# A fused spectral filter and MLP on one core: MLP steps taken two at a time

## The chip, the cores and the metric

The kernel runs on one core of a Trainium2 chip. The core has a matrix engine (TensorE, called PE in the profile, with its weight loads listed apart as PEld), a vector engine (VectorE, DVE), a scalar engine (ScalarE, ACT), GpSimd (POOL) and a queue engine that issues most of the transfers (SyncE, SP). Each engine works through its own list of instructions in order. The matrix engine writes its results into PSUM, of which this kernel uses eight banks of 512 float32 a partition; the other engines read them from there into SBUF.

The metric is the time of one execution on the device in microseconds. The output must agree with the reference in float32 accuracy: large products are made of three matmuls with operands split in a high and a low part.

## The reference

```
X  = rfft(x, axis=1)                       # x: 8 sequences of 3008 tokens, 256 wide
Yr = Xr @ w_r - Xi @ w_i + b_r
Yi = Xr @ w_i + Xi @ w_r + b_i
Y  = soft threshold of Yr and Yi by 0.01
y  = irfft(Y, n=3008, axis=1)
h  = y.reshape(24064, 256) @ w_in          # w_in: 256 x 2048
g  = maximum(0.01 * h, h)
out = g @ w_out                            # w_out: 2048 x 256
```

## The kernel before

The tokens of all sequences are handled in 47 chunks of 512. A sequence first goes through the transform stages: a forward transform in two parts (`fwd`, and `stage_b` in `mid`), the projection by w_r and w_i with bias and threshold (`proj`), and the inverse transform in two parts (`stage_g` in `mid`, and `inverse`), with trips through DRAM between them. `forms` then writes seven combinations of the four quarters of a chunk (two halves of the width by two halves of the tokens), each as a high and a low part (`yh`, `yl`).

The MLP takes a chunk in 8 steps, each for 256 of the 2048 hidden columns; there are 376 steps in all, counted by `i`, and (ci, q) is chunk and step in it. A step has three parts:

- `moe_a`: four of the seven products of a Strassen-like scheme, each three matmuls of 256 columns (L99, 12 matmuls), into two banks b1 and b2 of the PSUM tag `psh`, which has four banks. Then p1 is copied out of b1 (ACT, L614), u2 is summed (DVE, L615), and the first quarter of the activation's input is read out of b2 (DVE, L617 and L618).
- `moe_b`: the other three products (L99, 9 matmuls), into the same two banks. Then the DVE reads b2 for two more quarters (L630), ACT reads b1 through the activation (L632), applies it to the rest in SBUF (L633), and `halves` splits the result in `gh` (ACT, L597) and `gl` (DVE, L599). After L630 and L632 the two banks are free for another step.
- `moe_o`: the second product, for one half `eh` of the output columns, 6 matmuls of 512 columns (L646) from `gh` and `gl` into a bank of the tag `pso`, where all 8 steps of a chunk add up. After the last step of a chunk ACT copies the bank out (L651) and SP issues its transfer to DRAM (L652).

For the first chunk (`DIRECT = 1`) `moe_a` makes the plain products (12 matmuls of 512 columns) and `moe_b` does nothing.

The order in which each engine gets its instructions is set when the program is built, by a planner that goes through a simulated time: an engine takes the instruction that stands first in the traced program among those whose inputs and buffers are ready. Two things bind it. `in_order` queues every matmul of a part behind the matmul that was traced last in the part before, so the parts of the MLP follow each other in the order of the calls; within that bound single products may be put off. And the transform's TensorE work in the stage functions is queued behind the last MLP matmul traced at that point (`issue_after(mlp[0].ins)`).

`moe` is a generator. At each `yield` it gives its place in chunks, and the loop at the end of the kernel (L794 to L810) traces as much of the transforms of the next sequences as is due by that place. `tokens` traces the loads, the inverse transforms and `forms` of the next chunk in portions, one at each `next(nxt, None)`. Step i traces: moe_a of step i, moe_b of step i-1, a stop for the transforms, the second half of moe_o of step i-3, the first half of moe_o of step i-2, another stop. In the order of TensorE this is a, b, o, o for each step.

Buffers that bear on it: `psh` four banks, `pso` two and `psf` two (transforms); `gf`, `gh` and `gl` two buffers each; `u2` two, `p1` one.

Of the kernel before, what the change touches and what calls it, by code (L numbers as in the profile page):

```python
# [31 lines left out]
def spectral_mlp_kernel(  # L32
# [23 lines left out]
    NH = D // P  # L56
    NPAIR = NK1 // 2
    NQ = NF // 2
    NT, HT = 512, 256
    NV = 2 * NG * N1  # L60
    CS = 512
    LAG = 2
    PAUSE = 10 * CS
    DIRECT = 1
    SHARE = 1.7
# [25 lines left out]
    def in_order(part, *args):  # L91

        with tc.issue_after(mlp[0].ins) if mlp else nullcontext():
            part(*args)
# [559 lines left out]
    steps = [(ci, q) for ci in range(nch) for q in range(NQ)]  # L654
# [8 lines left out]
    def tokens(ci):  # L663

        yield
        for p in due[ci]:
            v_load(p)
        for _ in range(3):
            yield
        for eh in range(NH):  # L670
            for p in due[ci]:
                with tc.issue_after(mlp[0].ins):
                    inverse(p, eh)
                yield
        yield from forms(ci)

    def moe():

        for i, (ci, q) in enumerate(steps):
            if q == 0:  # L680
                nxt = tokens(ci + 1) if ci + 1 < nch else iter(())
            in_order(moe_a, ci, q)
            if i >= 1:
                in_order(moe_b, *steps[i - 1])
            next(nxt, None)
            yield ci + (q + 0.5) / NQ
            if i >= LAG + 1:
                in_order(moe_o, *steps[i - LAG - 1], 1)
            if i >= LAG:
                in_order(moe_o, *steps[i - LAG], 0)  # L690
            next(nxt, None)
            if q == NQ - 1:
                for _ in nxt:
                    pass
            yield ci + (q + 1) / NQ
        in_order(moe_o, *steps[-LAG - 1], 1)
        in_order(moe_b, *steps[-1])
        for s in steps[-LAG:]:
            for eh in range(NH):
                in_order(moe_o, *s, eh)  # L700

    class Stream:
        def __init__(self, gen, total):
# [90 lines left out]
    for i, pos in enumerate(moe()):  # L794
        if i % 2 == 0 and len(converted) < NQ:
            with tc.issue_after(made[0].ins), tc.issue_after(made[1].ins):
                next(wout, None)
        while cur + 1 < NB - 1 and pos >= (read[cur + 1] if cur >= 0 else 0):
            for s in streams:
                s.finish()  # L800
            cur += 1
            streams = ([Stream(fwd(cur + 1), (FWD + 4 * CS) * SHARE)] if cur else []) + [mids[cur]]
        frac = (pos - read[cur]) / (read[cur + 1] - read[cur]) if cur + 1 < NB else 1
        if cur == 0:
            frac = max(0, frac - 0.2) * 1.25
        work = frac / 0.95 * sum(s.total for s in streams)
        with tc.issue_after(converted[-1].ins) if cur == 0 else nullcontext():
            for s in streams:
                s.to(work / s.total)
                work = max(0, work - s.total)  # L810
# [106 lines left out]
```

## Time and profile before

| | us |
|---|---|
| median of three runs | 2535.69 |
| lowest and highest | 2535.54, 2536.94 |
| the profiled execution | 2536.52 |
| its span, first to last instruction | 2534.7 |
| PE busy | 2495.6 |
| DVE busy | 1872.9 |
| ACT busy | 1663.1 |

Busy times are unions of an engine's instructions. A matmul's duration in the profile is longer than the distance to the next one, since they overlap; distances are read from the starts. In the groups of a page the columns are busy time, mean duration in ns, and the idle time of the engine just before such instructions with what ended it.

### The profile page before, as it was taken

To read this page: it belongs to the slowest core of one execution; us is meant where nothing else is said; L and a number is where in the kernel's file an instruction comes from. 1 tells how busy PE (TensorE), PEld (TensorE's weight loads), DVE (VectorE), ACT (ScalarE), POOL (GpSimd) and SP (SyncE) were. 2 spreads that over 40 slices of the span, in tenths; PEclk is the share of its full clock that TensorE was granted. 3 is DMA by queue.
4 is the path that set the end of the run, shared out by engine and by line. 5 is a ranking of instruction groups with operands and counts; after the bars stand their busy time and mean duration, and the time that the engine had idled before them with its cause. 6 is when DMAs were issued, how large, how long until landed. Compare 5 with 4: busy or idle time off the path is not lost.

```text
span 2534.7 us, 42316 instructions
## 1 busy us (share of the span) xinstructions
PE 2495.6 (98%) x16180; PEld 2246.0 (89%) x16180; DVE 1872.9 (74%) x3460; ACT 1663.1 (66%) x3152; POOL 122.2 (5%) x96
## 2 busy tenths in 40 slices
PE   6999999999999999999999999999999999999999
PEld 4588888999899998999989999899998999999998
DVE  7886777777877778777777777877778777667665
ACT  4876765667666765667656676666765677656564
POOL 0000000000000000000000000000000010000000
PEclk8999999999999999999999999999999999999999
DMA  8621132111321113221132111321114211100000
GB/s 268 196 82 47 46 96 77 46 51 45 96 73 51 54 38 91 69 58 50 42 95 69 51 50 42 103 69 53 44 38 113 64 54 42 41 21 29 21 14 17
DMA packets 117803, 165.05 MB, mean 65 GB/s; under 512 B 13513, under 2 KB 69345, under 8 KB 117601
## 3 DMA queue, kind: packets, MB, share of 16 engines
q1 hardware_dynamic: 76228, 112.34, 14.6%
q10 hardware_dynamic: 41373, 50.01, 7.7%
q8 instruction: 127, 2.08, 0.3%
q14 instruction: 75, 0.61, 0.1%
HBM read 86.59 MB, written 75.71 MB: 64 GB/s over the span
## 4 chain that ended last, share of the span: by engine, by line
PE 93%; DMA 3%; ACT 2%; DVE 1%; issue 1%; SPq 0%; ACTq 0%; DVEq 0%
PE pso L646 40%; PE psh L99 35%; PE psf L85 11%; PE psf L518 3%; PE psf L373 3%; DMA xin<-x_dram 1%; DMA u_dram<-xin 1%; PE psh L85 0%; DMA u<-u_dram 0%; DVE gl L599 0%; DMA raw<-w_out_dram 0%; DMA bias<-b_i_dram 0%; ACT zf L429 0%; PE psh L373 0%; DMA win_raw<-w_in_dram 0%
## 5 line engine op out<-in xcount | busy, mean ns | idle before, releaser
L99 PE MATMUL psh<-yh,win_hi 128*128 128x256 f32 (+1 forms) x2608 | 728.7, 281 | 1.1 <-DVE gf L630 0.5
L99 PE MATMUL psh<-yl,win_hi 128*128 128x256 f32 (+1 forms) x2608 | 728.5, 280 | 0.0
L99 PE MATMUL psh<-yh,win_lo 128*128 128x256 f32 (+1 forms) x2608 | 723.5, 279 | 0.0
L599 DVE TENSOR_TENSOR gl<-gf,gh 128x1024 fp32r<-128x1024 f32 x376 | 461.3, 1227 | 299.8 <-ACT gh L597 289.6
L646 PE MATMUL pso<-gh,wout_hi 128*128 128x512 f32 x1504 | 592.9, 394 | 0.5 <-ACT ob L651 0.5
L646 PE MATMUL pso<-gl,wout_hi 128*128 128x512 f32 x1504 | 590.2, 392 | 1.3 <-DVE gl L599 1.3
L646 PE MATMUL pso<-gh,wout_lo 128*128 128x512 f32 x1504 | 589.3, 392 | 0.0
L99 PEld LDWEIGHTS psh<-yh,win_hi 128*128 128x128 f32 x2608 | 488.5, 188 | 19.6 <-DVE gf L630 2.2
L99 PEld LDWEIGHTS psh<-yl,win_hi 128*128 128x128 f32 x2608 | 490.2, 188 | 16.8 <-DVE yl L545 0.3
L99 PEld LDWEIGHTS psh<-yh,win_lo 128*128 128x128 f32 x2608 | 488.9, 188 | 1.9
L633 ACT ACTIVATE gf<-gf 128x768 f32<-128x768 f32 x368 | 311.8, 847 | 216.6 <-DVE gf L630 205.6
L597 ACT CAST gh<-gf 128x1024 fp32r<-128x1024 f32 x376 | 395.0, 1051 | 35.2 <-PE pso L646 25.9
L646 PEld LDWEIGHTS pso<-gl,wout_hi 128*128 128x128 f32 x1504 | 282.7, 188 | 63.0 <-DVE gl L599 4.0
L646 PEld LDWEIGHTS pso<-gh,wout_hi 128*128 128x128 f32 x1504 | 283.1, 188 | 47.0 <-ACT ob L651 0.9
L646 PEld LDWEIGHTS pso<-gh,wout_lo 128*128 128x128 f32 x1504 | 283.0, 188 | 46.5
L632 ACT ACTIVATE gf<-psh 128x256 f32<-128x256 f32 x368 | 142.2, 386 | 233.1 <-PE psh L99 225.3
L630 DVE TENSOR_TENSOR gf<-psh,u 128x512 f32<-128x512 f32 x368 | 252.4, 686 | 47.8 <-PE psh L99 46.3
L614 ACT COPY p<-psh 128x256 f32<-128x256 f32 x368 | 137.5, 374 | 143.9 <-PE psh L99 131.8
L411 POOL TENSOR_TENSOR kb<-bias,kc 128x512 f32<-128x512 f32 x84 | 119.5, 1423 | 2046.8 <-ACT kc L409 1800.4
L615 DVE TENSOR_TENSOR u<-psh,p 128x256 f32<-128x256 f32 x368 | 154.6, 420 | 32.9 <-ACT p L614 31.0
L617 DVE TENSOR_TENSOR gf<-psh,u 128x256 f32<-128x256 f32 x368 | 154.8, 421 | 21.1 <-PE psh L99 7.2
L618 DVE TENSOR_TENSOR gf<-psh,gf 128x256 f32<-128x256 f32 x368 | 154.5, 420 | 4.9
(124 smaller groups left out, 3124.5 us busy)
## 6 DMA issues: line engine op xcount, KB each, us to landing
u<-u_dram SPq DMA_DIRECT2D x192, 128.0 KB, 2.7
v_dram<-v ACTq DMA_DIRECT2D x192, 128.0 KB, 2.4
out_dram<-ob SPq DMA_DIRECT2D x94, 256.0 KB, 2.0
vin<-v_dram SPq DMA_DIRECT2D x96, 240.0 KB, 3.5
xin<-x_dram SPq DMA_DIRECT2D x78, 240.0 KB, 2.9
u_dram<-xin ACTq DMA_DIRECT2D x72, 240.0 KB, 2.4
raw<-w_out_dram SPq DMA_DIRECT2D x8, 512.0 KB, 4.7
win_raw<-w_in_dram SPq DMA_DIRECT2D x7, 512.0 KB, 6.8
```

Of the source, the lines that this page charges most:

```text
L85: last = nc.tensor.matmul(dst, a, b, start=(i == 0), stop=(i == len(terms) - 1))
L99: mlp[:] = [nc.tensor.matmul(dst, a, b, start=start and i == 0, stop=i == 2, skip_group_check=True)]
L597: cp = act.copy(gh, g)
L599: parted[:] = [cp, dve.tensor_sub(gl, g, gh.bitcast(F32))]
L614: act.copy(p1, b1[:, lo])
L615: dve.tensor_add(u2, b1[:, hi], p1)
L617: dve.tensor_add(g[:, 3], b2[:, hi], u2)
L618: dve.tensor_add(g[:, 3], b2[:, lo], g[:, 3])
L630: dve.tensor_add(g[:, 1:3], b2.rearrange("p (k n) -> p k n", k=2), u2.unsqueeze(1).broadcast_to([P, 2, HT]))
L632: act.activation(g[:, 0], b1[:, lo], AF.Prelu, alpha=SLOPE)
L633: act.activation(g[:, 1:4], g[:, 1:4], AF.Prelu, alpha=SLOPE)
L646: mlp[:] = [nc.tensor.matmul(po, a[:, f, s], r[:, i], start=(f == 0 and j == 0), stop=(f == NF - 1 and j == 2),)]
```

## The change

The steps are traced in pairs. For a pair i, i+1 the order of the calls becomes: moe_a of step i, moe_b of step i-1, a stop for the transforms, moe_a of step i+1, moe_b of step i, a stop, then both halves of moe_o of step i-2, a stop, both halves of moe_o of step i-1, a stop. In the order of TensorE this is a, b, a, b, o, o, o, o for two steps. The number of stops and the places that they give are the same, in the same sequence. The end of the generator follows suit: moe_b of the last step, then moe_o of the last two. The constant `LAG` is gone.

```diff
-        for i, (ci, q) in enumerate(steps):
+        def seconds(i):
+
+            for eh in range(NH):
+                in_order(moe_o, *steps[i], eh)
+
+        for i in range(0, len(steps), 2):
+            ci, q = steps[i]
             if q == 0:
                 nxt = tokens(ci + 1) if ci + 1 < nch else iter(())
-            in_order(moe_a, ci, q)
-            if i >= 1:
-                in_order(moe_b, *steps[i - 1])
-            next(nxt, None)
-            yield ci + (q + 0.5) / NQ
-            if i >= LAG + 1:
-                in_order(moe_o, *steps[i - LAG - 1], 1)
-            if i >= LAG:
-                in_order(moe_o, *steps[i - LAG], 0)
-            next(nxt, None)
-            if q == NQ - 1:
-                for _ in nxt:
-                    pass
-            yield ci + (q + 1) / NQ
-        in_order(moe_o, *steps[-LAG - 1], 1)
+            for k in range(2):
+                in_order(moe_a, *steps[i + k])
+                if i + k:
+                    in_order(moe_b, *steps[i + k - 1])
+                next(nxt, None)
+                yield ci + (q + (k + 1) / 2) / NQ
+            for k in range(2):
+                if i:
+                    seconds(i + k - 2)
+                next(nxt, None)
+                if k and q == NQ - 2:
+                    for _ in nxt:
+                        pass
+                yield ci + (q + (k + 3) / 2) / NQ
         in_order(moe_b, *steps[-1])
-        for s in steps[-LAG:]:
-            for eh in range(NH):
-                in_order(moe_o, *s, eh)
+        seconds(-2)
+        seconds(-1)
```

More of the change, by code (lines that the diff above doesn't have):

```diff
@@ L61, in spectral_mlp_kernel @@
     CS = 512
-    LAG = 2
     PAUSE = 10 * CS
```

## The prediction

> **What bounds the kernel now.** I read the page first, then the slices of 100 us, then the chain of waits, then the timeline around the change.
>
> ```profile
> span 2534.7 us, 42316 instructions
> PE 2495.6 (98%) x16180; PEld 2246.0 (89%) x16180; DVE 1872.9 (74%) x3460; ACT 1663.1 (66%) x3152; POOL 122.2 (5%) x96
> PEclk8999999999999999999999999999999999999999
> ```
>
> ```profile
> 0.00:100.00 100.00, 74.11 (x301) 51.68 (x302) 76.02 (x128) 59.37 (x110) 0.77 (x6) 0.93 0.79 230
> 200.00:300.00 100.00, 98.92 (x666) 90.43 (x665) 68.77 (x129) 67.09 (x134) 10.24 (x7) 0.98 0.17 48
> 1000.00:1100.00 100.00, 100.00 (x660) 90.86 (x659) 74.34 (x145) 63.58 (x122) 2.82 (x2) 1.00 0.26 77
> 2300.00:2400.00 100.00, 100.00 (x649) 90.78 (x648) 66.72 (x118) 59.46 (x99) 0.00 (x0) 1.00 0.07 21
> ```
>
> In the second fence the columns are the stretch, then the busy time of PE, PEld, DVE, ACT and POOL, the granted clock, the DMA share and GB/s. TensorE is idle for 39 us of 2534.7, and 26 of these lie in the first 100 us, ahead of most of the MLP. From then on it is full. So the change can gain next to nothing by closing gaps; it can only open some, or make the matmuls themselves follow each other faster.
>
> How fast they follow is read best where the transforms are over, in the chain of waits near 2303 us, one row for the first products and one for the second:
>
> ```profile
> 2303.24 2.41 PE psh L99 x21
> 2305.65 2.73 PE pso L646 x12
> ```
>
> One step costs 2.41 + 2.73 = 5.14 us of TensorE: 12 matmuls of moe_a, 9 of moe_b, 12 of moe_o. How many steps each stage holds follows from the second-product matmuls, 12 a step (first row); the second row is all of TensorE's work in the same stretch, the third the end stage:
>
> ```profile
> 311.50:2176.00 1864.50, 851.80 (x3398) 613.41 (x3399) 1.00 0.22 62
> 311.50:2176.00 1864.50, 1862.62 (x12358) 1697.70 (x12358) 1402.32 (x2630) 1242.67 (x2396) 107.27 (x80) 1.00 0.22 62
> 2176.00:2530.00 354.00, 196.15 (x808) 146.29 (x808) 1.00 0.07 23
> ```
>
> 3398 / 12 = 283 steps in the transform stage, each 1864.5 / 283 = 6.59 us, so 1.45 us a step is transform work; 808 / 12 = 67 steps in the end stage; 376 - 283 - 67 = 26 before, of which 8 are the direct ones without moe_b.
>
> **What the change moves.** It adds and removes no instruction. Per pair the queue goes from a, b, o, o, a, b, o, o to a, b, a, b, o, o, o, o. What counts is what each matmul run must wait for, and how much MLP work lies in front of it.
>
> *The banks of psh.* A step takes two of the four, from its moe_a until L630 (DVE, reads b2) and L632 (ACT, reads b1) of its moe_b are done. When a(i+1) starts, step i holds two, and step i-1 held the others: a(i+1) waits for L630 and L632 of b(i-1). Before, twelve second products stood between b(i-1) and a(i+1). After, nothing of the MLP does in the second step of each pair. The end stage shows the price, for the step whose nine b matmuls end at 2305.37:
>
> ```profile
> 2303.07 0.28 PE L99 MATMUL psh<-yh,win_hi 128*128 128x256 f32 x1
> 2303.67 0.28 PE L99 MATMUL psh<-yh,win_lo 128*128 128x256 f32 x1
> 2303.98 0.37 ACT L614 COPY p<-psh 128x256 f32<-128x256 f32 x1 [1.13 <-PE psh L99]
> 2304.80 0.28 PE L99 MATMUL psh<-yh,win_hi 128*128 128x256 f32 x1
> 2305.34 0.69 DVE L630 TENSOR_TENSOR gf<-psh,u 128x512 f32<-128x512 f32 x1
> 2305.37 0.28 PE L99 MATMUL psh<-yh,win_lo 128*128 128x256 f32 x1
> 2305.49 0.39 PE L646 MATMUL pso<-gh,wout_hi 128*128 128x512 f32 x1
> 2305.68 0.39 ACT L632 ACTIVATE gf<-psh 128x256 f32<-128x256 f32 x1 [1.33 <-PE psh L99]
> 2305.95 0.42 DVE L618 TENSOR_TENSOR gf<-psh,gf 128x256 f32<-128x256 f32 x1
> 2308.22 0.28 PE L99 MATMUL psh<-yh,win_hi 128*128 128x256 f32 x1
> ```
>
> TensorE could issue its next matmul at 2305.49. L632 ends at 2306.07 and L630 at 2306.03. What lies between such an end and the matmul that waited for it is seen here:
>
> ```profile
> 1005.45 1.22 DVE L599 TENSOR_TENSOR gl<-gf,gh 128x1024 fp32r<-128x1024 f32 x1
> 1006.80 0.41 PE L646 MATMUL pso<-gl,wout_hi 128*128 128x512 f32 x1
> ```
>
> ```profile
> PEld pso L646 <- DVE gl L599: 4.0, 8, 1.0
> ```
>
> In the timeline the weight load before that second row is marked as released by L599, whose end is 1006.67, so 0.13 us. In the new order a(i+1) would start at 2306.07 + 0.13 = 2306.20 instead of 2305.49: a gap of **0.71 us a pair** where nothing else is there to be issued. Today the next a comes only at 2308.22, 2.15 us after L632; that is the cover the change takes away. In the end stage the only other TensorE work are the inverse transforms of L518, four groups of eight in 100 us against ten pairs; I count no cover there (columns as above, L518 alone):
>
> ```profile
> 2300.00:2400.00 100.00, 4.22 (x32) 4.05 (x32) 1.00 0.07 21
> ```
>
> That makes 67 / 2 = 33 pairs x 0.71 = **23 us**.
>
> *The same in the transform stage.* Here the DVE also carries transforms, and L630 queues behind them. First and last step of the stage:
>
> ```profile
> 311.54 0.28 PE L99 MATMUL psh<-yh,win_lo 128*128 128x256 f32 x1
> 311.85 0.39 ACT L632 ACTIVATE gf<-psh 128x256 f32<-128x256 f32 x1 [0.31 <-PE psh L99]
> 313.72 0.68 DVE L630 TENSOR_TENSOR gf<-psh,u 128x512 f32<-128x512 f32 x1
> 2175.49 0.28 PE L99 MATMUL psh<-yh,win_lo 128*128 128x256 f32 x1
> 2175.83 0.68 DVE L630 TENSOR_TENSOR gf<-psh,u 128x512 f32<-128x512 f32 x1
> 2176.01 0.38 ACT L632 ACTIVATE gf<-psh 128x256 f32<-128x256 f32 x1
> ```
>
> From the end of the group's last matmul to the end of L630 it is 2.58 us in the first, 0.74 in the last; over all 284 groups of 21 in this stretch the mean is 1.15 (median 0.89), and for L632 0.29 (median 0.42). The b1 half of a(i+1), six matmuls or 0.70 us, can run once L632 is done and covers part of L630. Taken group by group (the earlier of the two, or the later less 0.70, whichever is more, with 0.075 us for the release and 0.165 because a matmul is issued that much before its predecessor's end), the gap averages 1.04 us. Against this stands that L630 will queue less: today L599 of the step before, 1227 ns, often stands ahead of it, and after the change that one belongs to the previous pair and ran during four halves of second products. I take 0.85, between the end stage's 0.71 and 1.04.
>
> ```profile
> L599 DVE TENSOR_TENSOR gl<-gf,gh 128x1024 fp32r<-128x1024 f32 x376 | 461.3, 1227 | 299.8 <-ACT gh L597 289.6
> L630 DVE TENSOR_TENSOR gf<-psh,u 128x512 f32<-128x512 f32 x368 | 252.4, 686 | 47.8 <-PE psh L99 46.3
> ```
>
> ```profile
> DVE gf L630 <- PE psh L99: 46.3, 65, 2.1
> PE psh L99 <- DVE gf L630: 0.5, 1, 0.5
> ```
>
> The last fence is from the table of waits (us in total, times, longest): only 65 of the 368 L630 found the DVE idle, and a's matmuls waited for one of them once.
>
> What can fill the gap is transform work: what is traced behind b(i-1) is queued behind its last traced matmul, so it becomes issuable just there. In the present trace a transform matmul stands directly behind 30% of the 284 groups, as after this one:
>
> ```profile
> 1014.51 2.42 PE psh L99 x21
> 1016.93 0.71 PE psf L85 x3
> ```
>
> Laid over the gaps, such matmuls fill 0.29 us of the 1.04 on the mean. So 0.85 - 0.30 = 0.55 us a pair: 283 / 2 = 142 pairs x 0.55 = **78 us**, and (26 - 8) / 2 = 9 earlier pairs, **5 us**. The bounds: all filled, 0 (then 5 us less as well); nothing filled at 1.04, 151 pairs = 157 us. I stay nearer the latter since 70% of groups have no transform matmul behind them and nothing of the MLP may pass: the second products are queued behind b(i), b(i) behind a(i+1).
>
> *The waits that become tighter or looser.* b(i), second of the pair, needs L618(i). In the end stage L618 ends 2306.37 - 2303.07 = 3.30 us after its a starts; b(i) comes 2.41 + 0.71 + 1.38 = 4.5 us after it: covered. If L618 is late, the three products of b1 and the second products pass. o(i-1) needs gl(i-1), from L599; for the first and the last group above that is
>
> ```profile
> 317.53 1.22 DVE L599 TENSOR_TENSOR gl<-gf,gh 128x1024 fp32r<-128x1024 f32 x1
> 2178.51 1.23 DVE L599 TENSOR_TENSOR gl<-gf,gh 128x1024 fp32r<-128x1024 f32 x1 [0.73 <-ACT gh L597]
> ```
>
> It ends 5.4 us after the group's last matmul on the mean of the 284, 7.3 us at the 95th percentile. On TensorE 0.7 of gap, 2.41 x 12 / 21 = 1.38 of a(i+1), 1.03 of b(i), 2.73 of o(i-2) and two matmuls, 0.46, lie between, 6.3 us, or 7.7 with the 1.45 of transforms: I count nothing; without the transforms a tenth of the pairs would lose up to 1 us, 18 us in all, for the upper bound. Buffers of gf, gh and gl (two each) come free later only for the second step, whose next reader is a whole run away. The output copies and their DMA move by half a step at most and the token loads on SP's queue keep their place among the four stops of a pair; nobody on the path waits for them.
>
> *The gain.* After a change from second to first products the first five matmuls come 0.120 us apart (2303.07 to 2303.67), the last five 0.114 (2304.80 to 2305.37): 0.03 us for each change. 180 of 368 changes go: **-6 us**. Beyond that no more than the 39 us of idle time could be gained, and nearly all of it lies in the head, which the change does not touch.
>
> Sum: 23 + 78 + 5 - 6 = 100 us. The profiled execution took 2536.5, its span 2534.7, the median of the runs is 2535.7; 2535.7 + 100 = **2636 us**, 3.9% slower. About 0.2%, 5 us, is what can be told from no change here.
>
> **The rivals.**
> 1. *Transforms fill every gap of their stage.* For it: they are 1.45 us a step, far more than the gap, and the planner takes whatever is ready. Against it: the 30%. Only the end stage pays: 23 - 6 = +17, 2553 us. Chance 0.14.
> 2. *Nothing fills, and gl is late too.* For it: DVE at 74% overall and only 65 of 368 L630 found it idle. 23 + 157 + 18 - 6 = +192, 2728 us. Chance 0.15.
> 3. *Not slower.* L630 and L632 would have to end before a(i+1) is due, or the planner would have to put 0.71 us of other work in front of it also in the end stage; then only the faster succession remains, 2536 - 6 = 2530 us. It decides from a release within 0.12 us of the last matmul on, and no row shows ACT's 0.39 us fitting there. Chance 0.05, with the case that the planner dissolves the pairs and nothing changes, 2536.
> 4. *The clock falls.* The first slice, with TensorE 74% busy, had 0.93 of the clock, the slice from 200 us, 99% busy, 0.98; those read from 300 us on 1.00. Gaps every 11 us at 0.98 over some 2400 us add 49 us to the forecast, 2685; at 0.93, 181 us, 2817. Against it: each gap is under 1 us. Chance 0.04. The Trainium skill, TensorE: Matmul & The Clock Gate, section "A second HAM failure mode: psum-queue depth-cycling", speaks for this one: frequent short idling between groups that cycle through banks made the clock gate swing. No slice of this trace shows it so far.
>
> **How the numbers follow.** The forecast has 0.62, the rivals 0.14, 0.15, 0.05 and 0.04. The range goes from 2552, which takes in most of rival 1, to 2722, the forecast with nothing filled at 1.04 us (2716) and a part of rival 2: 0.60 + 0.11 + 0.08 + 0.02, about 8 in 10. Slower by over 0.2%: 0.93; within 0.2%: 0.04; faster: 0.03.
>
> **What would show it.** In the chain of waits: pieces of 12 + 9 + 12 + 9 first products and 24 second ones in the end stage, with a wait of PE for L632 or L630 after the first 21, about 0.7 us each, 33 times; in the table of waits "PE psh L99 <- ACT gf L632" and "<- DVE gf L630" up from the 0.5 us above to 50 to 150 us. The slices from 2300 us fall from 100 to about 94 busy, those of the transform stage to about 96. If the end stage stays at 100, the bank argument is wrong; if it falls and the transform stage stays at 100, rival 1 holds; a PEclk below 1.00 after 300 us would be rival 4; waits of L646 for L599 of over 20 us, rival 2.

## The result, and the profile after

The changed kernel takes 2628.6 us in the median (four runs, 2624.8 to 2631.8) beside 2535.6 us for the kernel before on the same chip: 1.0367 times as long, 95% interval 1.0354 to 1.0380. The forecast was 2636 us. The profiled execution took 2628.4 us, its span is 2626.0.

The page after, its first lines and the groups that answer to those of before. One line fewer stands ahead of them in the code, so L99 is now L98, and likewise L645 is moe_o, L629 the DVE's reading of b2, L631 ACT's reading of b1, L598 makes gl.

```profile
span 2626.0 us, 42169 instructions
PE 2535.8 (97%) x16180; PEld 2259.3 (86%) x16180; DVE 1866.9 (71%) x3460; ACT 1654.8 (63%) x3152; POOL 117.2 (4%) x96
...
L98 PE MATMUL psh<-yh,win_hi 128*128 128x256 f32 (+1 forms) x2608 | 748.4, 287 | 52.4 <-DVE gf L629 26.2
...
L629 DVE TENSOR_TENSOR gf<-psh,u 128x512 f32<-128x512 f32 x368 | 252.4, 686 | 126.8 <-PE psh L98 124.8
```

TensorE has the same 16180 matmuls. Ahead of the first matmul of a product (the yh, win_hi row) it now stands idle for 52.4 us, where it was 1.1, as the same row of the page before shows:

```profile
L99 PE MATMUL psh<-yh,win_hi 128*128 128x256 f32 (+1 forms) x2608 | 728.7, 281 | 1.1 <-DVE gf L630 0.5
```

The table of waits after names who ended them (us in total, times, longest):

```profile
PE psh L98 <- DVE gf L629: 26.2, 41, 3.2
PE psh L98 <- ACT gf L631: 23.0, 49, 1.0
...
PE pso L645 <- DVE gl L598: 5.3, 13, 2.1
```

These are the two instructions that free a step's banks. One pair of the end stage, in rows picked from the timeline (start, duration, what, idle before and its releaser):

```profile
2380.23 0.69 DVE L629 TENSOR_TENSOR gf<-psh,u 128x512 f32<-128x512 f32 x1
2380.26 0.28 PE L98 MATMUL psh<-yh,win_lo 128*128 128x256 f32 x1
2380.57 0.38 ACT L631 ACTIVATE gf<-psh 128x256 f32<-128x256 f32 x1 [1.33 <-PE psh L98]
2380.98 0.38 PE L98 MATMUL psh<-yh,win_hi 128*128 128x256 f32 x1 [0.44 <-DVE gf L629]
2381.20 0.28 PE L98 MATMUL psh<-yl,win_hi 128*128 128x256 f32 x1
```

The last b matmul starts at 2380.26, the next first product at 2380.98: 0.72 us, of which 0.114 is the ordinary distance. And the chain of waits there, in order of time:

```profile
2380.23 0.70 DVE gf L629
2380.93 0.04 issue
2380.98 1.98 PE psh L98 x15
2382.96 1.38 PE pso L645 x6
2384.33 0.71 PE psh L98 x6
2385.05 4.09 PE pso L645 x18
2389.14 0.73 PE psh L98 x6
```

Behind the gap the planner does not keep the run of first products whole: six matmuls of the pair's second moe_b come only after six second products.

Where the 91 us of span went can be worked out from the starts of all matmuls in the two timelines: what a distance exceeds 114 ns after a matmul of 256 columns, 227 ns after one of 512 and 112 ns after one of 128 or 64 (the medians). Summed by the kind of matmul that came late, in us, with the distances that are less than 0.15 us too long in a column of their own:

| stage | late first products | late second products | late transforms | under 0.15 us each |
|---|---|---|---|---|
| transform stage, before (150 to 2180) | 1.4 | 3.2 | 3.8 | 23.6 |
| transform stage, after (150 to 2254) | 53.4 | 11.4 | 1.1 | 39.7 |
| end stage, before | 0.0 | 0.9 | 0.0 | 2.5 |
| end stage, after | 15.4 | 0.9 | 0.0 | 5.7 |

Together 35 us before and 128 us after; the first 150 us differ by less than 1. Of the 92 us between them 67 lie in first products that came late, 8 in second ones and 19 in the short ones; transforms give 3 back.

Most of the short ones belong to the waits too. In the rows above the matmul behind the one that waited follows it by 0.22 us and not by 0.114, and so it is behind each of the 102 late first products of this trace, by 0.11 us in the median: 11 of the 19 us. A wait costs its gap and 0.11 us more.

### The profile page after: what moved, and what is told of

It is laid out like the page before. It is cut to its first block, busy times and chain, and to the rows that moved or that the text cites. A ratio compares the mean times of both kernels' runs of the same rounds, so it can differ in the third digit from the quotient of the medians.

```text
span 2626.0 us, 42169 instructions
## 1 busy us (share of the span) xinstructions
PE 2535.8 (97%) x16180; PEld 2259.3 (86%) x16180; DVE 1866.9 (71%) x3460; ACT 1654.8 (63%) x3152; POOL 117.2 (4%) x96
## 4 chain that ended last, share of the span: by engine, by line
PE 79%; DVE 9%; ACT 6%; DMA 4%; issue 2%; ACTq 0%; SPq 0%; DVEq 0%
PE pso L645 34%; PE psh L98 28%; PE psf L84 10%; PE psf L517 3%; PE psf L372 2%; DVE gf L629 2%; DMA xin<-x_dram 2%; DVE gl L598 1%; DMA u_dram<-xin 1%; ACT zf L428 1%; DVE u L614 1%; ACT gf L631 1%; ACT zf L424 1%; DVE t L418 1%; ACT gf L632 1%
## 5 line engine op out<-in xcount | busy, mean ns | idle before, releaser
L98 PE MATMUL psh<-yh,win_hi 128*128 128x256 f32 (+1 forms) x2608 | 748.4, 287 | 52.4 <-DVE gf L629 26.2
L98 PE MATMUL psh<-yl,win_hi 128*128 128x256 f32 (+1 forms) x2608 | 730.6, 280 | 0.0
L98 PE MATMUL psh<-yh,win_lo 128*128 128x256 f32 (+1 forms) x2608 | 729.3, 280 | 0.0
L598 DVE TENSOR_TENSOR gl<-gf,gh 128x1024 fp32r<-128x1024 f32 x376 | 460.0, 1223 | 228.1 <-ACT gh L596 227.1
L645 PE MATMUL pso<-gl,wout_hi 128*128 128x512 f32 x1504 | 591.2, 393 | 5.8 <-DVE gl L598 5.3
L645 PE MATMUL pso<-gh,wout_hi 128*128 128x512 f32 x1504 | 592.5, 394 | 0.5 <-ACT gh L596 0.5
L645 PE MATMUL pso<-gh,wout_lo 128*128 128x512 f32 x1504 | 590.3, 392 | 0.0
L98 PEld LDWEIGHTS psh<-yh,win_hi 128*128 128x128 f32 x2608 | 489.5, 188 | 93.4 <-ACT gf L631 37.5
L98 PEld LDWEIGHTS psh<-yl,win_hi 128*128 128x128 f32 x2608 | 490.6, 188 | 14.4 <-DVE yl L544 0.3
L98 PEld LDWEIGHTS psh<-yh,win_lo 128*128 128x128 f32 x2608 | 490.7, 188 | 1.8
L632 ACT ACTIVATE gf<-gf 128x768 f32<-128x768 f32 x368 | 312.2, 848 | 259.4 <-DVE gf L629 239.6
L645 PEld LDWEIGHTS pso<-gl,wout_hi 128*128 128x128 f32 x1504 | 283.1, 188 | 70.5 <-DVE gl L598 13.0
L629 DVE TENSOR_TENSOR gf<-psh,u 128x512 f32<-128x512 f32 x368 | 252.4, 686 | 126.8 <-PE psh L98 124.8
L645 PEld LDWEIGHTS pso<-gh,wout_hi 128*128 128x128 f32 x1504 | 283.5, 188 | 49.8 <-ACT gh L596 1.3
L645 PEld LDWEIGHTS pso<-gh,wout_lo 128*128 128x128 f32 x1504 | 283.3, 188 | 48.7
L631 ACT ACTIVATE gf<-psh 128x256 f32<-128x256 f32 x368 | 142.5, 387 | 152.6 <-PE psh L98 149.6
```

Source lines behind the costliest of these rows:

```text
L98: mlp[:] = [nc.tensor.matmul(dst, a, b, start=start and i == 0, stop=i == 2, skip_group_check=True)]
L598: parted[:] = [cp, dve.tensor_sub(gl, g, gh.bitcast(F32))]
L629: dve.tensor_add(g[:, 1:3], b2.rearrange("p (k n) -> p k n", k=2), u2.unsqueeze(1).broadcast_to([P, 2, HT]))
L631: act.activation(g[:, 0], b1[:, lo], AF.Prelu, alpha=SLOPE)
L632: act.activation(g[:, 1:4], g[:, 1:4], AF.Prelu, alpha=SLOPE)
L645: mlp[:] = [nc.tensor.matmul(po, a[:, f, s], r[:, i], start=(f == 0 and j == 0), stop=(f == NF - 1 and j == 2),)]
```

## The experiments

The theory was that the four banks of psh set the loss: the second step's moe_a directly follows the moe_b whose banks it needs, and the transforms fill part of the gap. The main rival was that the pairing loses by its bursts: four halves of moe_o in a row want gl earlier, and DVE and ACT get their work in lumps. All runs (each interval is the ratio to the kernel before on the same chip):

| run | median us | against before, 95% interval |
|---|---|---|
| changed kernel | 2628.6 | 1.0354 to 1.0380 |
| moe_b's b1 product first, changed kernel | 2623.5 | 1.0330 to 1.0364 |
| the same, kernel before | 2543.5 | 1.0021 to 1.0045 |
| one half of moe_o between | 2562.1 | 1.0094 to 1.0125 |
| fifth bank for psh, one for pso | 2573.1 | 1.0137 to 1.0167 |
| its control, one bank for pso | 2628.6 | 1.0357 to 1.0388 |
| both halves together, not paired | 2556.6 | 1.0068 to 1.0098 |
| transforms traced at the gap alone | 2574.9 | 1.0141 to 1.0172 |
| transforms traced behind the first moe_o alone | 2681.4 | 1.0561 to 1.0597 |
| transforms at one stop a step, kernel before | 2558.3 | 1.0079 to 1.0106 |
| one half between, and transforms at that gap | 2544.8 | 1.0023 to 1.0049 |
| b, b, a, a, o, o, o, o | 2669.8 | 1.0510 to 1.0539 |
| the same, shifted by a step | 2619.8 | 1.0312 to 1.0340 |

**A fifth bank, and its control.** The output banks give one up: both halves of the columns are summed in one, so these two kernels leave the separate halves out. The diff shows the two lines that matter; the other users of the two tags, and the copies of the output, follow suit.

```diff
-            o_t[ci, eh] = bank("pso", 2)
+            o_t[ci, eh] = o_t[ci, 0] if eh else bank("pso", 1)
...
-        b1, b2 = bank("psh", 4), bank("psh", 4)
+        b1, b2 = bank("psh", 5), bank("psh", 5)
```

> The changed kernel with psh at five banks and pso at one: both halves of the output columns are summed in the same bank, so the output holds their sum twice; the copies and transfers of a chunk are all made after its last second product. Bank theory: the second step's a takes the free bank at once and needs one more only 0.70 us later; the gap in the end stage disappears, the waits of L98 for L631 and L629 fall below 10 us, and the time to 2545 to 2565 us (what is left is the wait for gl). Rival (bursts): 2620 to 2635 us, as with the one bank less alone.

> The control for the fifth bank: pso at one bank with the same sum of both halves, psh at four as in the changed kernel. Both theories: as the changed kernel, 2620 to 2640 us, if the single pso bank costs nothing by itself; what it differs from that is the price of the merging, to be taken off the run with five banks.

The control took 2628.6 us, as the changed kernel; with five banks it is 2573.1. So **one more bank takes away 55 us of the 93**. The end stage is full again, which it is not in the control's case (194.11 of 200 us); here the stretch of 2300 to 2500 us in the changed kernel, then with five banks (columns as in the prediction):

```profile
2300.00:2500.00 200.00, 194.15 (x1245) 174.70 (x1245) 129.50 (x234) 112.44 (x199) 0.00 (x0) 1.00 0.07 24
```

```profile
2300.00:2500.00 200.00, 200.00 (x1303) 182.50 (x1303) 136.89 (x245) 114.63 (x206) 0.00 (x0) 1.00 0.07 22
```

Waits of first products for L629 or L631 fall from 49.2 to 1.4 us. It is 8 us above what was expected; another wait grew, that for gl, threefold.

```profile
PE pso L645 <- DVE gl L598: 15.8, 20, 1.0
```

**Cover between the two.** One of the four halves of moe_o goes back between the first step's moe_b and the second step's moe_a.

```diff
                 yield ci + (q + (k + 1) / 2) / NQ
+                if i and k == 0:
+                    in_order(moe_o, *steps[i - 2], 0)
             for k in range(2):
                 if i:
-                    seconds(i + k - 2)
+                    for eh in range(1 - k, NH):
+                        in_order(moe_o, *steps[i + k - 2], eh)
```

> The changed kernel with one of the four halves of moe_o (6 matmuls, 1.38 us) put back between the first step's b and the second step's a: a, b, o, a, b, o, o, o. Bank theory: the banks are released 0.5 us after b in the end stage and 1.3 us on the mean in the transform stage, so the waits of L98 for L631 and L629 (49 us for the matmuls alone) go to under 15 us; gl of the later step is needed as early as before, so some wait of L645 for L598 stays, 5 to 20 us: 2545 to 2565 us. Rival (bursts): three halves in a row and the same pairing, 2605 to 2630 us.

2562.1 us, as the bank theory had it, and the same wait is the largest that is left:

```profile
PE pso L645 <- DVE gl L598: 14.4, 19, 1.7
...
PE psh L98 <- DVE gf L629: 6.1, 6, 2.2
```

**The other part alone.** In the kernel before, not paired, both halves of a step's moe_o come one after the other.

```diff
-            if i >= LAG + 1:
-                in_order(moe_o, *steps[i - LAG - 1], 1)
             if i >= LAG:
-                in_order(moe_o, *steps[i - LAG], 0)
+                for eh in range(NH):
+                    in_order(moe_o, *steps[i - LAG], eh)
```

> The kernel before, not paired, with both halves of moe_o of the same step one after the other (a, b, o, o of step i-2) in place of the second half of step i-3 and the first of step i-2. It takes one part of the change alone: gl must be ready one half and one step's stretch earlier, 5.6 us of MLP work after its b in place of 7.0, while the banks have the cover they had. Bank theory: little, 2536 to 2552 us, all of it waits of L646 for L599. Rival (the loss comes from gl being needed earlier): most of the loss is here already, 2590 to 2630 us.

2556.6 us, 21 us above the kernel before and 5 above the range. The loss is in one wait, and late second products account for 20 us of it in the timeline:

```profile
PE pso L646 <- DVE gl L599: 13.4, 24, 2.9
```

So the rival has a share: to want gl earlier costs about 20 us where nothing else delays TensorE. In the changed kernel late second products are only 8 us more than before; that the gaps ahead of moe_a give gl the time there is likely, but was not tried apart. Of the 37 us left with five banks, 18 are late second products, 9 late first ones and 9 short distances; that is why 55 us, and not 93, come back. The two costs do not add.

**The release of b1 earlier.** The product into b1 is made first of the three.

```diff
+        product(b1[:, lo], ci, q, 2)
+        two = list(mlp)
         product(b2[:, hi], ci, q, 4)
         product(b2[:, lo], ci, q, 3)
-        product(b1[:, lo], ci, q, 2)
+        mlp[:] = two
```

> The changed kernel with the three products of moe_b in another order: first the one into b1 (product 2), then the two into b2. The instructions are the same. Bank theory (a of the second step of a pair waits for L631 on b1 and L629 on b2 of the step before): b1 comes free about 0.7 us earlier, so the b1 half of a starts at once and its 0.70 us run beside L629; the b2 half waits 0.2 to 0.3 us at most. The gap of 0.72 us in the end stage falls to 0.3 or less, the time to 2585 to 2605 us. Rival (the loss comes from the bursts that pairing makes, with gl late for moe_o and the DVE and ACT loaded in lumps): when b1 comes free changes nothing, 2625 to 2633 us.

> The kernel before with the same edit as above: moe_b's product into b1 first. In the kernel before 12 second products lie between b and the next a, so no theory expects a wait to change: 2530 to 2541 us. If it is faster or slower by more, the order of moe_b's products has a price of its own that has nothing to do with the pairs.

A miss: 2623.5 us, 5 less than the changed kernel, not 24 to 44, though also just below the rival's range; and in the kernel before the edit costs 8 us, 2543.5. In the end stage it did what was expected. The b1 half now runs on behind the b matmuls (27 in a row), and the b2 half waits 0.18 us (2385.19 to 2385.48 in the timeline, less 0.114):

```profile
2382.29 3.18 PE psh L98 x27
2385.47 0.01 issue
2385.48 1.33 PE psh L98 x9
```

Late first products of the end stage fall from 15.4 to 4.6 us. In the transform stage they stay at 52 us (53 before the edit). There L629 decides, and the edit makes its products 0.35 us later: from the end of the first step's moe_b to the end of L629 it is 1.27 us on the mean of 142 pairs, 0.99 without the edit, while L631 moved from 0.66 to 0.11 ahead of that end. Here the wait for ACT has gone over to the DVE (L631 and L633 in this kernel are L629 and L631 above):

```profile
PE psh L98 <- DVE gf L631: 33.9, 40, 2.2
...
PE psh L98 <- ACT gf L633: 5.0, 13, 0.8
```

**What fills the gap.** The transforms after the first sequence are traced at one of a pair's four stops only: behind the first step's moe_b (0, as in the diff), or behind the first two halves of moe_o (2 in its place).

```diff
+        if cur > 0 and i % 4 != 0:
+            continue
         frac = (pos - read[cur]) / (read[cur + 1] - read[cur]) if cur + 1 < NB else 1
```

> The changed kernel, but the transforms of the sequences after the first are traced at one of the four stops of a pair alone, the one behind b of the first step, where the gap is. The work is the same. If transform matmuls fill the gap because they become issuable just there, more pairs have one behind that b: the waits of L98 for L631 and L629 in the transform stage fall by half or more, 2580 to 2605 us. If what fills the gaps is chance (work that became ready anyway) and the DVE's queue gets longer by the lump, no gain or a loss: 2625 to 2660 us.

> As the run before, but traced at the stop behind the first two halves of moe_o alone, far from the gap. If filling depends on the stop, fewer gaps are filled: the waits of L98 for L631 and L629 rise, 2640 to 2680 us. If the stop does not matter for the gap but the DVE is freer of transform work when L629 is due, they fall: 2600 to 2625 us.

2574.9 against 2681.4 us: the same work, and 107 us between two places to trace it. Counted in the timelines of the transform stage, some other work stands between the first step's moe_b and the second step's moe_a in 93% of the pairs with the stop at the gap, 76% in the changed kernel and 38% with the stop elsewhere. The waits for the banks, first at the gap, then elsewhere:

```profile
PE psh L98 <- DVE gf L629: 22.5, 43, 1.6
...
PE psh L98 <- ACT gf L631: 5.6, 9, 1.7
```

```profile
PE psh L98 <- ACT gf L631: 63.5, 95, 2.0
PE psh L98 <- DVE gf L629: 32.7, 57, 2.1
```

The first is 5 us better than its range, the second 1 us above its own. The end stage, which has no such transforms, keeps its 15.3 us in both. Whether tracing at one place costs by itself was asked of the kernel before, with one stop a step instead of two:

```diff
+        if cur > 0 and i % 2:
+            continue
```

> The kernel before with its transforms (after the first sequence) traced at one of its two stops a step, the one behind b. It has no gap to fill. If the place of the stop matters through the gap alone, nothing changes: 2530 to 2541 us. If lumping transforms helps or harms by itself, it shows here, and the two runs on stops are to be corrected by it.

A miss: 2558.3 us. Lumps cost 23 us there, in waits for gl and for the bank:

```profile
PE pso L646 <- DVE gl L599: 6.9, 13, 1.0
PE psh L99 <- DVE gf L630: 5.7, 9, 1.4
```

Tracing at one stop has a price of its own, then. How large it is in pairs was not measured; the 54 us gained at the gap came in spite of whatever it is, and it may be part of the 53 lost elsewhere.

**Both together.**

> Two of the edits above together on the changed kernel: one half of moe_o between the first step's b and the second step's a, and the transforms of the sequences after the first traced at the one stop behind that b. If bank waits and their filling explain the loss, what is left is the wait for gl, and transform matmuls between b and the next half of moe_o give gl more time: 2538 to 2560 us, below the 2562 us of the half alone. If transforms in one lump cost by themselves, 2565 us or more.

2544.8 us, within the range. Late first products are 3.8 us, late second ones 10.8. This is the best of the paired kernels, and it is still 0.36% above the kernel before.

**Pairs without the neighbours.** Four parts in another order: both moe_b, then both moe_a, then the four halves of moe_o of steps i-3 and i-2.

```diff
             for k in range(2):
-                in_order(moe_a, *steps[i + k])
-                if i + k:
-                    in_order(moe_b, *steps[i + k - 1])
+                if i:
+                    in_order(moe_b, *steps[i + k - 2])
+                if k:
+                    in_order(moe_a, *steps[i])
+                    in_order(moe_a, *steps[i + 1])
...
-                if i:
-                    seconds(i + k - 2)
+                if i + k - 3 >= 0:
+                    seconds(i + k - 3)
```

> Pairs kept, with 42 first products and 24 second ones in a row, but the run begins with both moe_b: b of steps i-2 and i-1, then a of steps i and i+1, then both halves of moe_o of steps i-3 and i-2. The banks of step i-2 have 9 matmuls (1.03 us) until a(i) wants them, those of step i-1 have 12 (1.38 us); gl is wanted a whole run later than in the changed kernel. Bank theory: no gap in the end stage, where the release comes 0.5 us after b; waits of L98 under 15 us, of L645 under 5; half the changes between first and second products save at most 6 us: 2530 to 2552 us. Rival (bursts of 42 and 24 are what costs): 2590 to 2635 us.

A clear miss, 2669.8 us. Within a chunk it does what was expected, and the planner keeps the runs whole:

```profile
2327.88 4.79 PE psh L98 x42
2332.67 5.45 PE pso L645 x24
2338.12 4.81 PE psh L98 x42
```

4.79 + 5.45 = 10.24 us a pair, where two steps of the kernel before take 10.28. But a new wait has come in:

```profile
PE pso L645 <- ACT ob L650: 58.9, 50, 3.2
```

With even i, steps i-3 and i-2 are, in every fourth run, the last of a chunk and the first of the next. The next chunk's second products come directly behind those that finish the bank, and the bank must be copied out first: by the timeline 77 us of lateness lie in the first twelve second products of the chunks, 69 of them ahead of the first into each bank. It is the same mechanism as the one under study, moved to pso. The pairs shifted by one step tell:

```diff
-        for i in range(0, len(steps), 2):
-            ci, q = steps[i]
+        for i in range(-1, len(steps), 2):
+            if i + 1 < len(steps):
+                ci, q = steps[i + 1]
...
```

> The run of b, b, a, a, o, o, o, o once more, with the pairs shifted by one step, so that the last two steps of a chunk make their second products in the same run and a whole run of first products lies between them and those of the next chunk. In the run before this one, 77 us of the waits lay ahead of the first second product of a chunk, where pso must first be copied out (L650). Theory (the banks alone, psh in the changed kernel and pso here, set what a run must wait for): these waits go, waits of L645 for L650 under 5 us, 2550 to 2600 us; what stays are the 40 us ahead of first products, where L629 and L631 come late behind transform work. Rival (long runs cost by themselves): 2640 to 2675 us. Faster than the kernel before only if these 40 us go too, which nothing in the edit does.

2619.8 us: 50 less, and the waits for L650 fall from 58.9 to 1.5 us. That part holds, late second products fall from 81 to 5.5 us. But it is 20 us above the range, because late first products rose from 41 to 76 us:

```profile
PE psh L98 <- DVE gf L629: 36.0, 33, 2.6
PE psh L98 <- ACT gf L631: 20.6, 24, 1.2
```

What such a wait is made of shows in the chain of waits at the start of a chunk, in the end stage:

```profile
2312.41 1.41 PE psh L98 x12
...
2314.23 0.85 ACT gf L632
2315.08 0.26 ACT p L613
2315.34 0.96 ACT gh L596
2316.29 0.02 issue
2316.32 1.23 DVE gl L598
2317.54 0.61 DVE gf L629
2318.16 0.04 issue
2318.20 0.96 PE psh L98 x6
```

L629, which frees the bank, stands on the DVE behind L598, and L598 waits for ACT's gh. The planner fixed that order. Why it does so there and seldom in the kernel before was not tried; for these two orders the lateness of first products in the transform stage stays open.

## Why the prediction was right

The mechanism is the one that was predicted, at the place where it was predicted. That the sum came within 7 us of the 93 measured is in part luck: its terms were off both ways.

**The bound** was read rightly: TensorE was all but full from the head on, there was next to nothing to gain, and the gaps are paid in full (92 us of lateness, 91 us of span).

**The banks.** Step a(i+1) waits for L630 and L632 of b(i-1): shown, by the releasers of the waits, by the fifth bank (55 us less) and by the half of moe_o put between (66 us less). The Trainium skill, Perfetto Trace Analysis, section "Optimization Strategy", reads a gap that repeats on the engine that should be full as a possible sign that SBUF or PSUM has no room for the next tile; the run with five banks agrees, with 55 us less.

**The end stage.** Worked out were 0.71 us a pair; the gap in the rows above is 0.72 from start to start, 0.61 more than the ordinary distance. The step that was too large is the 0.13 us from a release to the matmul: here the matmul starts 0.03 us after the end of L631 (2380.57 + 0.38). The 0.11 us that the matmul behind it loses were not in the sum; by luck the two make up for each other, and a wait costs 0.72 us in all. "I count no cover" for L518 was wrong too: 25 of 32 pairs have the wait, the others have L518 in front. So it is 15.4 us and 3.2 in short ones, against 23.

**The transform stage.** 83 us were forecast with the early pairs; late first and second products and short distances came to 53.4 + 11.4 + 39.7 - (1.4 + 3.2 + 23.6) = 76 us. The sum was better than its terms. The share of gaps with something to fill them was put at 30%, from what followed b in the kernel before, and it was 76%; the likely reason is that a gap lets in what becomes ready in it, which the trace before, without gaps, can't show. Against that, the price of a gap was taken too low and a filled gap was taken as closed. By the starts of the matmuls from the end of moe_b to the end of moe_a, 35 pairs with nothing in the gap lost 1.11 us each, nearer to the 1.04 worked out than to the 0.85 taken, and the 116 pairs with something in it still lost 0.29 us each: 39 + 33 = 72 us in place of 83. The rest of a filled gap shows in the late first products: of their 53.4 us, 21.3 lie ahead of the second step's moe_a and 29.6 in its middle, where its products go over to the other bank; 21 of these 38 waits are ended by L631, 17 by L629. That one half of moe_a runs while the other bank is still read, as forecast, is so; it does not cover all of the reading. And "I count nothing" for gl was too little by 8 us here (1.4 of them at the lower clock told of below), by 16 to 18 where the gaps are taken away (one half between, five banks).

**The gain** of 6 us from fewer changes between first and second products didn't come. They were to be halved; direct ones from second to first products, which the sum had priced, went from 277 to 226 only (from first to second, from 300 to 256), since b products are put off behind second ones, as in the chain after. Short distances grew in place of shrinking, by what follows each wait above all.

**The signs and the range.** The waits for L631 and L629 came to 49 us, just under the 50 to 150 named; TensorE was 97% busy from 2300 us on (194.15 of 200), not 94. The 2716 us for nothing filled is some 6 us too high by its own terms: 23 + 157 - 6 above 2535.7 makes 2710. It changes nothing here.

**The rivals.** Transforms fill everything (1): refuted, though by tracing them at the gap the time goes more than half of the way. Nothing fills (2) and not slower (3): refuted. The clock (4): it fell twice, for 1.6 us each time, as told below, and did not stay down. The Trainium skill, TensorE: Matmul & The Clock Gate, section "A second HAM failure mode: psum-queue depth-cycling", describes such swings for short idling; the regular gaps of 0.6 us left the clock at 1.00 (the row of 2300 to 2500 us), and the two swings followed gaps of 3.4 and 2.7 us.

## What to carry to other kernels

When the order of work is changed on an engine that is full, ask for each run which buffers it needs, who frees them, and how much work lies between that one and the run: the cover that the old order gave is what the new one takes away. A new order can bring the same wait back at another buffer and another place (here psh within a pair, pso between chunks), so go through all pools at all boundaries. And where gaps are filled by other work, the place at which that work is let in can matter as much as the gap: 107 us between two places here.

## What the runs showed of the hardware

After some gaps TensorE ran at half its clock for one stretch of 3.41 us. Its longest gap in the changed kernel is ended here. The DVE had sat idle for 2.96 us ahead of L269, for a reason that the profile does not name, and L629 had its turn only behind it and three others (the rows are picked):

```profile
662.54 0.28 PE L98 MATMUL psh<-yh,win_lo 128*128 128x256 f32 x1
662.63 0.69 DVE L269 TENSOR_TENSOR xs<-xin,xin 120x512 f32<-120x512 f32 x1 [2.96 <-issue]
665.31 0.68 DVE L629 TENSOR_TENSOR gf<-psh,u 128x512 f32<-128x512 f32 x1
666.05 0.39 PE L98 MATMUL psh<-yh,win_hi 128*128 128x256 f32 x1 [3.23 <-DVE gf L629]
```

The stretches ahead of the gap, around it and behind it, with the granted clock third from the right:

```profile
659.00:662.40 3.40, 3.40 (x28) 3.28 (x28) 0.67 (x2) 1.49 (x4) 0.00 (x0) 1.00 0.82 228
662.40:666.20 3.80, 0.57 (x5) 0.38 (x4) 3.57 (x6) 0.66 (x3) 0.00 (x0) 1.00 0.00 1
667.40:670.70 3.30, 3.30 (x9) 2.54 (x8) 2.08 (x3) 0.84 (x2) 0.00 (x0) 0.50 0.00 0
```

Over the traces of all 14 kernels, behind the first 150 us, such a stretch came with 4 of 38 gaps of 1.5 to 2 us, 11 of 17 of 2 to 2.5, 3 of 4 of 2.5 to 3 and 11 of 12 of 3 to 3.5 (a gap is what a distance exceeds the ordinary one). It began between 0.5 us ahead of the gap's end and 1.6 us behind it. Worked out, it costs up to 3.41 x 0.5 = 1.7 us beside the gap itself; by the starts of the matmuls the two in the changed kernel cost 1.6 each. In the first of the two orders with both moe_b in front there are ten, up to 17 us of its loss. Three more came without a gap of that length close ahead, and why is open.

The matmul behind one that waited comes late as well. Over the same 14 traces there are 709 first products that start 0.15 us or more late; behind 699 of them the next matmul follows 0.09 to 0.12 us later than its ordinary 0.114. What causes it was not tried.
